# Gated linear attention with a soft mixture of experts: exchanging the two heads in half of y^T

## The chip, the cores and the metric

The kernel runs on one core of a Trainium2 chip. The metric is the device time of one execution in microseconds; the median of three runs of the kernel before is 186.47 us (186.04 to 186.61). A core has a matrix engine (TensorE, "PE" in the profile; its weight loads are listed as "PEld"), a vector engine (VectorE, DVE), a scalar engine (ScalarE, ACT), GpSimd (POOL), and a sync engine (SyncE, SP) that here issues all transfers. They work side by side and wait for each other by semaphores. Matrix results land in PSUM, whose banks hold 512 fp32 columns in each of 128 partitions; everything else is in SBUF.

## The reference

Everything is fp32. For each of 4 batches and 8 heads, over 768 tokens of head dimension 48:

```python
f = 1.0 / (1.0 + np.exp(-f_logit))
for t in range(S):
    state = f[:, :, t, :, None] * state + np.einsum('bhd,bhe->bhde', k[:, :, t], v[:, :, t])
    y[:, :, t] = np.einsum('bhd,bhde->bhe', q[:, :, t], state)
```

The eight heads of a token are put side by side into x, [3072 tokens, 384]. Then a soft mixture with 8 experts of 4 slots each (32 slots, hidden size 1024):

```python
logits = x @ phi                                   # [3072, 32]
d = softmax(logits, over tokens);  slot_input = d.T @ x
h = np.maximum(slot_input[e] @ w1[e], 0.0);  slot_out[e] = h @ w2[e]
c = softmax(logits, over slots);   out = c @ slot_out   # [3072, 384]
```

## The kernel before

The recurrence is done in chunks of 128 tokens (six chunks, `NM`), two heads at a time: 16 pairs of heads, four to a batch. Of a pair, head 0 lies in partitions 0 to 47 and head 1 in partitions 64 to 111 of 112. For each pair:

- the decays: e, ln, the scan `L` (`Lb`), g, p on ScalarE and VectorE, k and q scaled on GpSimd (`kb`, `qb`);
- `kt`: k turned to tokens by partitions, six transposes (L337), copied out by VectorE;
- `score` (L349): per chunk and head k^T q, with the 48 dimensions of a head in the rows, masked by VectorE into `scb`;
- `kv` (L377): the state that each chunk adds; `state` (L381) scans over chunks on VectorE into `sb`;
- `intra` (L368): y^T of each chunk from v and the masked scores, added up in PSUM with
- `inter` (L390): y^T from the state before the chunk and q, chunks 1 to 5, two heads each. Head r has its operands in rows 64r to 64r+47 and its output in partitions 64r to 64r+47;
- `y_copy`: y^T to `yT` in SBUF; `logits` (L413): phi times y^T, four groups of 192 tokens (a chunk and a half) in four strips of 32 output partitions, added up over the four pairs of a batch; `x_tr` (L401) and `x_copy`: y turned to tokens by partitions (`xb`).

Per batch follow the maximum and exponential of the logits, `l_tr` (twice: "te" for the weights of the slot inputs, "tl" for the softmax over slots), `slots_in` (L457, the slot inputs), a running join of the batches on VectorE, and the softmax over slots (`c_max` to `c_div`), which `c_tr` turns into `cT`. As a group of 192 tokens is a chunk and a half, `l_tr` does two transposes and two products with picked columns of the identity.

After the last batch comes the ending: `up` (L580), `turn`, `down` (L624) over all experts, and `combine` (L669), whose results are copied to a staging buffer and stored in two halves of 192 columns, six stores for each half.

The order of the work is written by a planner (`Plan`): each step is declared with an engine, an estimated duration, what it reads and writes, and a due time. Up to the last pair the order on each engine is that of the due times; loads on SP and the whole ending are ordered by simulated time. PSUM is divided into three buffers "a" of two banks and two buffers "b" of one bank; a step takes a free one by name, and the steps that read it free it. A mode such as "rows", "quarters" or "square" beside a step's name is the shape of tiles it uses on TensorE, for which the planner charges a change.

Of the kernel before, what the change touches and what calls it, by code (L numbers as in the profile page):

```python
# [28 lines left out]
PIECE = 768  # L29
HALF = DM // 2  # L30

# [170 lines left out]
def gla_soft_moe_kernel(ctx: ExitStack, tc: tile.TileContext, q, k, f, v, vt, phi, w1, w2, out):  # L202
# [46 lines left out]
    el = P([128, NM, NS], "el")  # L249
    ce = P([128, NM, NS], "ce")  # L250
    cm = P([128, NM], "cm")
    cT = P([128, 6, 128], "cT")
# [7 lines left out]
    phs = P([PW, PPB, NS], "phs")  # L260
# [16 lines left out]
    for t in pbx:  # L277
        nc.vector.memset(t[:, :, NM - 1], 0.0)

# [82 lines left out]

    def intra(o, i, h):
        u = unit(("y", i)) if h == 0 else un["y", i]
        for m in range(3 * h, 3 * h + 3):
            for r in range(2):
                vv = vb[i % N_V][:, m].rearrange("p r e -> p (r e)")[:, D * r : D * r + (D if r else 64)]
                nc.tensor.matmul(  # L368
                    u[rows(r), C * m : C * m + C], vv, scb[i % N_SC][:, r, h, m % 3],
                    start=m in (0, 4), stop=False, skip_group_check=True,  # L370
                )
# [13 lines left out]
    def inter(o, i):  # L385
        u = un["y", i]
        for m in range(1, NM):
            for r in range(2):
                rs = slice(64 * r, 64 * r + D)
                nc.tensor.matmul(  # L390
                    u[rs, C * m : C * m + C], sb[i % N_S][rs, :, m - 1], qb[i % N_Q][rs, C * m : C * m + C],
                    start=False, stop=m in (3, NM - 1), skip_group_check=True,
                )

    def y_copy(o, i):
        copy(o, yT[i % N_Y][:PW], un["y", i][:PW, :S])
# [6 lines left out]
    def x_copy(o, i):  # L403
        b, p = divmod(i, PPB)
        dst = xbs[b % 2][:, :, 96 * p : 96 * p + 96].rearrange("p m (r e) -> p m r e", r=2)
        copy(o, dst, un["xt", i][:, :S].rearrange("p (m r e) -> p m r e", m=NM, r=2)[:, :, :, :D])


    def logits(o, i):
        b, p = divmod(i, PPB)  # L410
        u = unit(("pl", b)) if p == 0 else un["pl", b]
        for g in range(4):
            nc.tensor.matmul(  # L413
                u[32 * g : 32 * g + 32, :192], phs[:, p], yT[i % N_Y][:PW, 192 * g : 192 * g + 192],
                start=p == 0, stop=p == PPB - 1, skip_group_check=True,
            )
# [11 lines left out]
    def l_tr(o, src, key):  # L428

        u = unit(key)  # L430
        pick = ident.rearrange("p (a b s) -> p a b s", a=2, b=2)
        nc.tensor.transpose(u[:, 0:128], src[:, 0:128], ident)
        nc.tensor.transpose(u[:, 224:352], src[:, 64:192], ident)
        for b, cs in ((0, slice(128, 192)), (1, slice(0, 64))):
            half = slice(64 * b, 64 * b + 64)
            nc.tensor.matmul(
                u[half, 128:256].rearrange("p (a x) -> p a x", a=2)[:, :, :NS], src[:, cs], pick[:, :, b], start=True, stop=True,
            )

    def by_block(key):  # L440
        return un[key][:, :384].rearrange("p (n a x) -> p a n x", n=3, a=2)[:, :, :, :NS]

    def blocks(t):
        return t.rearrange("p (a n) s -> p a n s", a=2)

    def el_copy(o, key):
        copy(o, blocks(el), by_block(key))

    def slots_in(o, b, key, rounds=(0, 1)):
# [3 lines left out]
        for x in rounds:  # L453
            for g in range(4):
                half = slice(64 * (g % 2), 64 * (g % 2) + 64)
                ws, n = (half, 1 + 3 * (g // 2)) if x else (slice(0, 128), 2 * (g % 2) + 3 * (g // 2))
                nc.tensor.matmul(u[32 * g : 32 * g + 32, :DM], el[ws, n], xb[ws, n], start=x == 0, stop=x == 1)  # L457
# [25 lines left out]
    def c_max(o, key):  # L483
        nc.vector.reduce_max(cm.rearrange("p (a n) -> p a n", a=2), by_block(key), axis=AX.X)

    def c_sub(o, key):
        m = cm.rearrange("p (a n) -> p a n", a=2).unsqueeze(3).broadcast_to([128, 2, 3, NS])
        nc.vector.tensor_tensor(blocks(ce), by_block(key), m, op=ALU.subtract)
# [4 lines left out]
    def c_sum(o):  # L493
        nc.vector.reduce_sum(cm, ce, axis=AX.X)
        nc.vector.tensor_scalar(cm, cm, 1e-9, None, op0=ALU.add)
        nc.vector.reciprocal(cm, cm)  # L496

    def c_div(o):
        nc.gpsimd.tensor_tensor(ce, ce, cm.unsqueeze(2).broadcast_to([128, NM, NS]), op=ALU.mult)  # L499

    def c_tr(o, b, key):

        u = unit(key)
        nc.tensor.transpose(u[:, :128], flat(ce)[:, :128], ident)
        if b % 2:
            nc.tensor.matmul(u[64:, 128:256], flat(ce)[:, 128:], ident, start=True, stop=True)
        else:
            nc.tensor.transpose(u[:64, 128:256], flat(ce)[:, 128:], ident)

    def c_copy(o, b, key):  # L510
        u = un[key]
        copy(o, cT[:, b], u[:, :128])
        rs = slice(64 * (b % 2), 64 * (b % 2) + 64)
        copy(o, cT[rs, 4 + b // 2], u[rs, 128:256])
# [141 lines left out]
    of = out.rearrange("b n p d -> p (b n) d")  # L656

    def staged(k0, k1):
        t = w1b[4 + k0 // 8]
        return t[:, 2 * HALF * (k0 % 8) : 2 * HALF * ((k1 - 1) % 8 + 1)].rearrange("p (n d) -> p n d", d=HALF)  # L660

    def combine(o, hh, u2):

        u = unit(("pf", hh, u2)).rearrange("p (n d) -> p n d", n=2)
        b, x = divmod(u2, 3)
        for n in range(2):
            g = 2 * x + n if x < 2 else 2 * (b % 2) + n
            gs = slice(32 * g, 32 * g + 32)
            nc.tensor.matmul(  # L669
                u[:, n, :HALF], cT[gs, b if x < 2 else 4 + b // 2], s4[gs, HALF * hh : HALF * hh + HALF],  # L670
                start=True, stop=True,
            )

    def out_copy(o, hh, u2):
        n = 12 * hh + u2
        copy(o, staged(n, n + 1), un["pf", hh, u2].rearrange("p (n d) -> p n d", n=2)[:, :, :HALF])

    def store(o, hh, u0, u1):
        n = 12 * hh
        nc.sync.dma_start(of[:, 2 * u0 : 2 * u1, HALF * hh : HALF * hh + HALF], staged(n + u0, n + u1))  # L680
# [10 lines left out]
    def attention(i):  # L691
# [17 lines left out]
        op("dk", {"POOL": 1.84}, decay_k, i, r=[G, K], w=[K], due=z - 2 * T + 3.8)  # L709
# [13 lines left out]
        op(("ie", "quarters"), {"PE": 1.13}, inter, i, r=[Q, SB, YY], w=[YY], due=z + 2.2, ni=40)  # L723
# [5 lines left out]
    def soft(b, z):  # L729

        CT, tl = ("ct", b), ("tl", b)
        op(("tl", "square"), {"PE": 0.35}, l_tr, lt, tl, r=["lt"], w=[tl], due=z[0], take=[(tl, "a")], ni=12)
# [5 lines left out]
        op(("ct", "square"), {"PE": 0.35}, c_tr, b, CT, r=["ce"], w=[CT], due=z[1], take=[(CT, "a")], ni=6)  # L738
# [4 lines left out]
    def mixture(b, z):  # L743
# [8 lines left out]
        op(("te", "square"), {"PE": 0.35}, l_tr, et, key, r=["et"], x=["el"], w=[key], due=z + T + 4, take=[(key, "b")], ni=12)  # L752
# [7 lines left out]
        op(("pi", "strips"), {"PE": 1.3}, slots_in, b, key, r=[*XB[b], "el"], w=[key], due=z + 3 * T + 3.5, take=[(key, "b")], ni=32)  # L760
# [6 lines left out]
    op("lphi", {"SP": 0.45}, load, phs, phi, w=["phs"], due=5, kb=56)  # L767
# [57 lines left out]
    op(("pi", "strips"), {"PE": 1.3}, slots_in, L, PI, r=[*XB[L], "el"], w=[PI], due=z + 2, take=[(PI, "b")], ni=32)  # L825
# [31 lines left out]
    for hh in range(2):  # L857
# [10 lines left out]
        for u2 in range(12):  # L868
            b, x = divmod(u2, 3)
            key, d2 = ("pf", hh, u2), d + 5 + 0.3 * u2  # L870
            cts = [("cT", b)] if x < 2 else [("cT", 2 * (b // 2)), ("cT", 2 * (b // 2) + 1)]
            op("comb", {"PE": 0.35}, combine, hh, u2, r=[("s4", hh), *cts], w=[key], due=d2, take=[(key, "a")], ni=8)
# [129 lines left out]
```

## Time and profile before

| | us |
|---|---|
| median of three runs | 186.47 |
| profiled execution | 185.44 |
| its span, first to last instruction | 183.6 |
| TensorE busy | 159.2 |
| VectorE / ScalarE / GpSimd busy | 108.3 / 95.7 / 93.1 |
| score, both calls (L349) | 27.3 |
| intra (L368) / inter (L390) | 25.8 / 21.4 |
| kv (L377) / kt (L337) / xt (L401) | 15.0 / 13.3 / 12.0 |
| logits (L413) / slot inputs (L457) | 8.5 / 6.5 |

The lower rows are TensorE's busy times by line over the whole span; overlapping instructions count once. The span leaves out what lies before the first and behind the last instruction, 1.8 us. The profile names lines as L390, an instruction's tiles as out<-in, and x20 is a count of instructions. An fp32 product appears as two matmul records, a transpose as one. In the chain of work that ended last, pieces follow each other in time, each with its start and length; "issue" is time in which an engine waited for nothing that the profile shows.

### The profile page before, as it was taken

Reading aid. Unit: us, or ns where it says so; the run is one execution under the profiler, and the core shown is the slowest. Engines: PE = TensorE matmul, PEld = TensorE weight load, DVE = VectorE, ACT = ScalarE, POOL = GpSimd, SP = SyncE. Lnnn points to the kernel's source line nnn. Section 1 sums busy time; section 2 is a strip of 40 time slices with the busy share of each in tenths; the row PEclk is TensorE's granted clock in tenths of the full one; section 3 lists DMA queues with packets and bytes.
Section 4 is the critical chain, followed back from the end, with each engine's and each line's share of the span. In section 5 each row is a group of like instructions: output and inputs, shape, how many; then the busy total and the mean of one; then the engine's idle time right before and its main releaser. Section 6 shows DMA issues by size and latency. Waiting matters only on the chain.

```text
span 183.6 us, 5864 instructions
## 1 busy us (share of the span) xinstructions
PE 159.2 (87%) x2468; PEld 123.2 (67%) x2468; DVE 108.3 (59%) x154; ACT 95.7 (52%) x171; POOL 93.1 (51%) x88
## 2 busy tenths in 40 slices
PE   0049999999899999999999999999999999997800
PEld 0049889889688796898876888878645446665600
DVE  2669878678977684889967677749261113032300
ACT  4975666856777466695775663512252211052610
POOL 2199999988657939676896788520101000000000
PEclk9999999999999999999999999999999999999985
DMA  5999999999999999997566459999996194059691
GB/s 197 378 405 379 303 349 346 411 398 401 390 396 398 396 403 396 397 321 231 170 209 177 153 153 289 354 376 388 384 381 263 25 305 190 4 167 301 213 315 54
DMA packets 24931, 54.00 MB, mean 294 GB/s; under 512 B 2256, under 2 KB 8512, under 8 KB 24896
## 3 DMA queue, kind: packets, MB, share of 16 engines
q1 hardware_dynamic: 24896, 53.54, 81.7%
q8 instruction: 21, 0.34, 0.8%
q14 instruction: 14, 0.11, 0.2%
HBM read 48.82 MB, written 4.72 MB: 292 GB/s over the span
## 4 chain that ended last, share of the span: by engine, by line
PE 81%; issue 5%; DVE 3%; DMA 2%; POOL 2%; ACT 2%; SPq 0%; DVEq 0%; POOLq 0%; ACTq 0%
PE sc L349 14%; PE y L368 12%; PE y L390 10%; PE kv L377 7%; PE po L624 6%; PE up L580 6%; PE kt L337 5%; PE xt L401 5%; PE pl L413 4%; PE pf L669 4%; PE pi L457 3%; DMA kb<-in_k_dram 2%; DVE same L284 1%; PE turn L597 1%; ACT w1b L295 1%
## 5 line engine op out<-in xcount | busy, mean ns | idle before, releaser
L319 POOL TENSOR_TENSOR kb<-kb,gb 112x768 f32<-112x768 f32 x16 | 40.0, 2500 | 16.8 <-ACT gb L312 15.7
L309 DVE TENSOR_TENSOR_SCAN Lb<-starts,fb 112x768 f32<-112x768 f32 x16 | 29.9, 1870 | 5.7 <-ACT fb L305 5.6
L323 POOL TENSOR_TENSOR qb<-qb,pb 112x768 f32<-112x768 f32 x16 | 29.6, 1851 | 5.9 <-ACT pb L315 5.9
L354 DVE TENSOR_TENSOR scb<-sc,mask 128x768 f32<-128x768 f32 x32 | 29.1, 950 | 5.5 <-PE sc L349 5.4
L295 ACT COPY yT<-y 112x768 f32<-112x768 f32 x16 | 12.8, 799 | 34.6 <-PE y L390 34.6
L349 PE MATMUL sc<-qb,kb 48*128 48x128 f32 x384 | 27.3, 290 | 2.3 <-issue 1.2
L349 PEld LDWEIGHTS sc<-qb,kb 48*128 48x128 f32 x384 | 24.1, 196 | 5.1 <-issue 1.8
L368 PE MATMUL y<-scb,va 128*48 128x128 f32 (+1 forms) x384 | 25.8, 278 | 0.1
L295 DVE COPY kta<-kt 128x672 f32<-128x672 f32 x16 | 13.7, 853 | 19.8 <-PE kt L337 19.8
L337 PE MATMUL kt<-ident,kb 112*128 112x112 f32 x96 | 13.3, 277 | 11.2 <-POOL kb L319 11.2
L368 PEld LDWEIGHTS y<-scb,va 128*64 128x64 f32 (+1 forms) x384 | 21.9, 131 | 0.4 <-issue 0.2
L390 PE MATMUL y<-qb,sb 48*48 48x128 f32 x320 | 21.4, 277 | 0.0
L390 PEld LDWEIGHTS y<-qb,sb 48*48 48x48 f32 x320 | 17.9, 160 | 2.7 <-DVE sb L381 2.2
L337 PEld LDWEIGHTS kt<-ident,kb 112*128 112x128 f32 x96 | 9.9, 146 | 14.4 <-POOL kb L319 11.5
L499 POOL TENSOR_TENSOR ce<-ce,cm 128x192 f32<-128x192 f32 x4 | 4.6, 1154 | 21.8 <-DVE cm L496 13.8
L305 ACT ACTIVATE fb<-fb,one 112x768 f32<-112x768 f32 x16 | 15.0, 937 | 0.6
L377 PE MATMUL kv<-va,kta 128*64 128x48 f32 (+1 forms) x384 | 15.0, 225 | 0.0
L302 ACT ACTIVATE fb<-fb 112x768 f32<-112x768 f32 x16 | 13.4, 840 | 2.9 <-DMA fb<-in_f_dram 2.9
L377 PEld LDWEIGHTS kv<-va,kta 128*64 128x64 f32 (+1 forms) x384 | 13.0, 135 | 2.0 <-issue 0.2
L332 POOL COPY pbx<-pb 112x240 f32<-112x240 f32 x16 | 14.3, 892 | 0.0
L315 ACT ACTIVATE pb<-Lb 112x768 f32<-112x768 f32 x16 | 13.5, 845 | 0.0
L295 ACT COPY xb<-xt 128x576 f32<-128x576 f32 x16 | 10.2, 638 | 6.2 <-PE xt L401 6.2
(145 smaller groups left out, 245.7 us busy)
## 6 DMA issues: line engine op xcount, KB each, us to landing
w1b<-in_w_dram SPq DMA_DIRECT2D x34, 384.0 KB, 6.8
fb<-in_f_dram SPq DMA_DIRECT2D x16, 384.0 KB, 6.1
kb<-in_k_dram SPq DMA_DIRECT2D x16, 384.0 KB, 6.6
qb<-in_q_dram SPq DMA_DIRECT2D x16, 384.0 KB, 6.2
va<-in_v_dram SPq DMA_DIRECT2D x16, 288.0 KB, 6.3
out_dram<-w1b SPq DMA_DIRECT2D x12, 384.0 KB, 4.0
scb<-in_w_dram SPq DMA_DIRECT2D x4, 384.0 KB, 6.3
fb<-in_w_dram SPq DMA_DIRECT2D x3, 384.0 KB, 4.6
```

The lines of the kernel that those rows point to most:

```text
L295: {"ACT": nc.scalar.copy, "DVE": nc.vector.tensor_copy, "POOL": nc.gpsimd.tensor_copy}[o.eng](dst, src)
L305: nc.scalar.activation(fb[i % N_F][:PW], fb[i % N_F][:PW], AF.Ln, bias=one[:PW])
L309: nc.vector.tensor_tensor_scan(Lb[i % N_L][:PW], flat(starts)[:PW], fb[i % N_F][:PW], 0.0, op0=ALU.mult, op1=ALU.add)
L319: nc.gpsimd.tensor_tensor(t, t, gb[i % N_G][:PW], op=ALU.mult)
L323: nc.gpsimd.tensor_tensor(t, t, pb[i % N_P][:PW], op=ALU.mult)
L332: nc.gpsimd.tensor_copy(pbx[i % N_S][:PW, :, : NM - 1], ends(i)[:, : NM - 1].unsqueeze(1).broadcast_to([PW, D, NM - 1]))
L337: nc.tensor.transpose(u[:, C * m : C * m + PW], kb[i % N_K][:PW, C * m : C * m + C], ident[:PW, :PW])
L349: nc.tensor.matmul(u[:, 512 * r + C * m : 512 * r + C * m + C], kb[i % N_K][rs, cs], qb[i % N_Q][rs, cs], start=True, stop=True,)
L354: nc.vector.tensor_tensor(scb[i % N_SC][:, :, h], un["sc", i, h].rearrange("p (r x) -> p r x", r=2)[:, :, : 3 * C].rearrange("p r (m t) -> ...
L368: nc.tensor.matmul(u[rows(r), C * m : C * m + C], vv, scb[i % N_SC][:, r, h, m % 3], start=m in (0, 4), stop=False, skip_group_check=True,)
L377: nc.tensor.matmul(u[rows(r), :, m], ktb[i % N_KT][:, m, rows(r)], vb[i % N_V][:, m, r], start=True, stop=True)
L390: nc.tensor.matmul(u[rs, C * m : C * m + C], sb[i % N_S][rs, :, m - 1], qb[i % N_Q][rs, C * m : C * m + C], start=False, stop=m in (3, NM ...
```

## The change

In chunks 0 to 2 the two heads change places in y^T: head 0 goes to partitions 64 to 111, head 1 to 0 to 47. `intra` writes them there, and `inter` does so too, so its products use the tiles (rows 0-63 to columns 64-127) and (rows 64-127 to columns 0-63) in chunks 1 and 2 and the two others in chunks 3 to 5, in the order 1, 3, 2, 4, 5. y in PSUM has three chunks in each bank (before: four and two).

What reads y^T has to follow. phi is loaded in two versions (112 KB, before 56 KB), with the heads either way. The two odd groups of 192 tokens are put into another order, the whole chunk first and the shared half chunk behind, so `logits` writes them in two products. Now the second half of each group is a half chunk, `l_tr` is three plain transposes; the weights get eight blocks of 32 columns (before six), of which the softmax over slots zeroes the unused halves with a mask `valid`. `slots_in` undoes the exchange: the two groups of exchanged chunks are written as two products of half the columns each. `c_tr` is always two transposes, `c_copy` one copy instead of two. `combine` takes whole chunks by 32 rows as before and shared chunks by 64 rows. The output is laid out as [128, 2, 24, 192], so that a store writes 3072 adjacent bytes per partition; the host puts the tokens back in order. The tl turn takes a buffer b instead of a, and some planned durations differ.

```diff
+SWAP = NM // 2
+WHOLE, SHARED = (0, 2, 3, 5), (1, 4)
...
+    el = P([128, 2, 4, NS], "el")
+    ce = P([128, 8, NS], "ce")
+    cT = P([128, B, 2, 128], "cT")
...
+    nc.gpsimd.memset(valid, 1.0)
+    nc.gpsimd.memset(valid[64:, 4:8:2], 0.0)
+    nc.gpsimd.memset(valid[:64, 5:8:2], 0.0)
...
     def intra(o, i, h):
...
             for r in range(2):
+                at = 1 - r if m < SWAP else r
+                v0 = 576 * (i % N_V) + 96 * m + D * r
                 nc.tensor.matmul(
-                    u[rows(r), C * m : C * m + C], vv, scb[i % N_SC][:, r, h, m % 3],
-                    start=m in (0, 4), stop=False, skip_group_check=True,
+                    u[rows(at), y_cols(m)], va[:, v0 : v0 + (D if at else 64)], scb[i % N_SC][:, r, h, m % 3],
+                    start=m % 3 == 0, stop=False, skip_group_check=True,
                 )
...
     def inter(o, i):
-        for m in range(1, NM):
+        for m in (1, 3, 2, 4, 5):
             for r in range(2):
                 rs = slice(64 * r, 64 * r + D)
+                at = 64 * (1 - r if m < SWAP else r)
                 nc.tensor.matmul(
-                    u[rs, C * m : C * m + C], sb[i % N_S][rs, :, m - 1], qb[i % N_Q][rs, C * m : C * m + C],
+                    u[at : at + D, y_cols(m)], sb[i % N_S][rs, :, m - 1], qb[i % N_Q][rs, C * m : C * m + C],
...
     def logits(o, i):
-        for g in range(4):
-            nc.tensor.matmul(
-                u[32 * g : 32 * g + 32, :192], phs[:, p], yT[i % N_Y][:PW, 192 * g : 192 * g + 192],
+        for x in range(2):
+            for g in range(4):
+                t = 192 * g
+                to, at, n = (0, t + 64, C) if g % 2 else (0, t, 192)
+                if x:
+                    if g % 2 == 0:
+                        continue
+                    to, at, n = C, t, 64
+                nc.tensor.matmul(
+                    u[32 * g : 32 * g + 32, to : to + n], phs[:, int(g < 2), p], yT[i % N_Y][:PW, at : at + n],
...
     def l_tr(o, src, key):
         nc.tensor.transpose(u[:, 0:128], src[:, 0:128], ident)
-        nc.tensor.transpose(u[:, 224:352], src[:, 64:192], ident)
-        for b, cs in ((0, slice(128, 192)), (1, slice(0, 64))):
-            nc.tensor.matmul(
-                u[half, 128:256]..., src[:, cs], pick[:, :, b], start=True, stop=True,
-            )
+        nc.tensor.transpose(u[:, 128:256], src[:, 64:192], ident)
+        nc.tensor.transpose(u[:64, 128:256], src[:, 128:192], ident)
...
     def slots_in(o, b, key, rounds=(0, 1)):
...
         for x in rounds:
+            for r in range(2):
+                for g in range(4):
+                    ws, n = (half, SHARED[g // 2]) if x else (slice(0, 128), WHOLE[g])
+                    dst, src = u[32 * g : 32 * g + 32, :DM], xb[ws, n]
+                    if g < 2:
+                        dst = dst.rearrange("p (w r e) -> p w r e", w=PPB, r=2)[:, :, r]
+                        src = src.rearrange("p (w r e) -> p w r e", w=PPB, r=2)[:, :, 1 - r]
+                    elif r:
+                        continue
+                    nc.tensor.matmul(dst, el[ws, x, g], src, start=x == 0 and r == 0, stop=x == 1, skip_group_check=True)
...
     def c_sum(o):
+        nc.vector.tensor_tensor(cm, cm, valid, op=ALU.mult)
...
     def c_tr(o, b, key):
-        nc.tensor.transpose(u[:, :128], flat(ce)[:, :128], ident)
-        if b % 2:
-            nc.tensor.matmul(u[64:, 128:256], flat(ce)[:, 128:], ident, start=True, stop=True)
-        else:
-            nc.tensor.transpose(u[:64, 128:256], flat(ce)[:, 128:], ident)
+        for x in range(2):
+            nc.tensor.transpose(u[:, 128 * x : 128 * x + 128], flat(ce)[:, 128 * x : 128 * x + 128], ident)
...
+    def store(o, hh, u2):
+        nc.sync.dma_start(out[:, hh, 2 * u2 : 2 * u2 + 4], staged(hh, u2, 2))
...
-        op("dk", {"POOL": 1.84}, decay_k, ...
+        op("dk", {"POOL": 2.5}, decay_k, ...
-        op(("ie", "quarters"), {"PE": 1.13}, inter, ...
+        op(("ie", "quarters"), {"PE": 0.72}, inter, ...
-        op(("tl", "square"), {"PE": 0.35}, l_tr, ..., take=[(tl, "a")], ni=12)
+        op(("tl", "square"), {"PE": 0.35}, l_tr, ..., take=[(tl, "b")], ni=6)
-    op("lphi", {"SP": 0.45}, load, phs, phi, w=["phs"], due=5, kb=56)
+    op("lphi", {"SP": 0.45}, load, phs, phi, w=["phs"], due=5, kb=112)
```

The path for large decays (`general`), which these inputs do not take, is adapted in the same way.

114 lines of the change are left out of this document (51 added, 63 removed).

## Prediction

> **What bounds the kernel now.** I read the page first: the busy shares, the slices and the chain that ended last.
>
> ```profile
> span 183.6 us, 5864 instructions
> PE 159.2 (87%) x2468; PEld 123.2 (67%) x2468; DVE 108.3 (59%) x154; ACT 95.7 (52%) x171; POOL 93.1 (51%) x88
> PE   0049999999899999999999999999999999997800
> PE 81%; issue 5%; DVE 3%; DMA 2%; POOL 2%; ACT 2%; SPq 0%; DVEq 0%; POOLq 0%; ACTq 0%
> ```
>
> TensorE (PE) is busy in nearly every slice from the fourth to the 38th and owns 81% of the chain. Only the start (waiting for the first loads and elementwise work) and the end (draining stores) lie outside it. So I next read the chain in order of time, one steady pair of heads:
>
> ```profile
> 75.93 1.27 PE y L390 x20
> 77.19 0.46 PE pl L413 x8
> 77.66 0.73 PE kt L337 x6
> 78.38 0.57 PE xt L401 x6
> 78.96 1.54 PE sc L349 x24
> 80.49 0.77 PE kv L377 x21
> 81.26 1.39 PE y L368 x24
> 82.65 1.27 PE y L390 x20
> ```
>
> A pair takes 6.72 us (75.93 to 82.65) and consists of TensorE work without a hole; the first number is the start, the second the length on the chain. What is taken off a TensorE piece here comes off the time, 16 times, until another engine's loop becomes the longer one.
>
> **The inter products, 16 times.** Ten fp32 products are 20 matmul records. Head 0 now goes from rows 0-47 to output partitions 0-47, head 1 from rows 64-111 to partitions 64-111: the diagonal pair of 64x64 tiles only. Narrow windows of the timeline show what runs at once:
>
> ```profile
> 75.86 0.46 PE L390 MATMUL y<-qb,sb 48*48 48x128 f32 x4
> 75.86 0.57 PE L390 MATMUL y<-qb,sb 48*48 48x128 f32 x6
> 77.12 0.37 PE L413 MATMUL pl<-yT,phs 112*32 112x192 f32 x4
> 69.87 0.53 PE L457 MATMUL pi<-xb,el 64*32 64x384 f32 x4
> 72.17 0.38 PE L349 MATMUL sc<-qb,kb 48*128 48x128 f32 x2
> ```
>
> Two more records of the inter product lengthen the stretch by 0.11 us (first two rows): one round of the two diagonal tiles. Five products per tile are ten rounds, 1.10 of the 1.27 us; 0.17 is entry. After the change chunks 1 and 2 leave crosswise and chunks 3 to 5 straight, in the order 1, 3, 2, 4, 5, so the straight tiles have three products (six rounds) and the crossed ones two, beside them: 0.17 + 6 x 0.11 = 0.83 us, 0.44 less.
>
> Do four such tiles run together? The last three rows are the nearest. Four records of column strips stand in 0.37 us, though one alone takes 0.34 (the mean of that group below): all four at once. The 64x32 records of the slot inputs run four at once with two row halves, so two tiles that share rows but not columns do not exclude each other. The score's two row halves write the same partitions in two banks at once, so sharing columns does not either. The new y also has chunks 0 to 2 in one bank and 3 to 5 in the other. Bounds per pair: 0 (no overlap) and 0.63, if 20 records go at the pace of kv, 24 in 0.77 us. I take 0.44, since no row suggests a third tile would wait: **-7.0 us**.
>
> The Trainium skill speaks against this: "TensorEngine Tiling (Array Packing)", Restrictions and Gotchas, says that different row tiles cannot access the same PSUM bank simultaneously. Chunks 1 and 2 send both row halves to one bank, so by that rule two of the four tiles would wait and the term would be about 0. But the kernel does so already: both heads of a chunk go to one bank in different partitions, and four records stand in 0.46 us above, two per round. The trace does not bear the rule out for disjoint partitions.
>
> **Extra records.** The logits get 12 records instead of 8: strips 1 and 3 split 192 columns into 128 and 64 because their halves need different head orders. Slot inputs get 24 instead of 16 with half the columns in strips 0 and 1.
>
> ```profile
> L413 PE MATMUL pl<-yT,phs 112*32 112x192 f32 x128 | 8.5, 338 | 0.0
> ```
>
> No strip streams more columns than before, and the strips overlap, so the lower bound is 0. The upper one is four (eight) records at a serial transpose's 0.12 us (kt: six in 0.73), 0.48 and 0.96. It is nearest to the lower one; I take 0.05 per logits and 0.1 per slot input: 16 x 0.05 + 4 x 0.1 = **+1.2 us**.
>
> **Turning the logits and weights, plain transposes.** Eight turns (tl and te, four batches) lose four matmul records with 64 columns and get one transpose; two of four ct turns lose a two-record matmul.
>
> ```profile
> 61.44 0.26 PE tl L432
> 61.81 0.27 PE tl L436 x4
> 62.08 0.73 PE kt L337 x6
> 70.97 0.11 PE ct L508
> 71.08 0.58 PE kt L337 x6
> 101.26 0.36 PE ct L506 x2
> ```
>
> The removed group costs 0.27, and kt behind it takes 0.73 against 0.58 behind a 64-wide transpose (ct L508), the form that is added at 0.11: 0.27 - 0.11 + 0.15 = 0.31, times 8 = **-2.5**. The odd ct gives 0.36 - 0.11 + 0.15 = 0.40, twice: **-0.8**. Bounds for the two together: 0.16 and 0.25 alone, if the 0.15 has another reason (-1.8), to the -3.3 taken.
>
> **The PSUM buffer of tl.** It moves from the three large buffers (a) to the two small ones (b). Today tl, kt and xt hold all three when the scores want one:
>
> ```profile
> PE sc L349 <- issue: 1.2, 3, 0.4
> 62.84 0.86 DVE L295 COPY kta<-kt 128x672 f32<-128x672 f32 x1 [1.77 <-PE kt L337]
> 63.80 1.61 PE L349 MATMUL sc<-qb,kb 48*128 48x128 f32 x24 [0.42 <-issue]
> 63.99 0.36 DVE L488 TENSOR_TENSOR ce<-tl,cm 128x192 f32<-128x192 f32 x1
> ```
>
> The scores start 0.10 after kt's copy ends (63.70), with 0.42 idle; three such places, 1.2 us. With one large buffer free they go: **-1.2**. In b, tl lies between two kv products and must be read by c_sub before the next one; c_sub is done at 64.35 (last row), a microsecond before the scores end and kv begins (63.80 + 1.61). If that cover were gone, kv would wait for the rest of the DVE work.
>
> **What is late next.**
>
> ```profile
> L309 DVE TENSOR_TENSOR_SCAN Lb<-starts,fb 112x768 f32<-112x768 f32 x1 | 1.7, 1733 | 0.0
> L381 DVE TENSOR_TENSOR_SCAN sb<-kv,pbx 112x288 f32<-112x288 f32 x1 | 0.7, 747 | 0.0
> L354 DVE TENSOR_TENSOR scb<-sc,mask 128x768 f32<-128x768 f32 x32 | 29.1, 950 | 5.5 <-PE sc L349 5.4
> ```
>
> VectorE's loop per pair (the Lb scan 1.73, kt copy 0.86, two masks 1.90, state scan 0.75; means in the rows) is 5.3 us. The circle from one state scan to the next runs over inter 0.83, logits 0.51, kt 0.73, xt 0.57, half a score 0.77, two masks and the scan: 6.1 us and some 0.1 for handovers, against a new pair of 6.72 - 0.44 + 0.05 = 6.33. It just fits, so part of the gain comes back wherever VectorE has more to do:
>
> ```profile
> PE sc L349 <- DVE kta L295: 0.7, 1, 0.7
> 83.92 1.72 DVE L464 TENSOR_TENSOR nmb<-nmx,nmb 128x1 f32<-128x1 f32 x1
> 116.97 1.50 DVE L474 SCALAR_TENSOR_TENSOR sms<-sms,nmb 128x1 f32<-128x1 f32 x1
> 53.55:83.91 30.36, 29.94 (x484) 24.87 (x486) 21.44 (x27) 20.90 (x36) 23.33 (x27) 1.00 1.01 378
> 83.91:114.61 30.70, 30.28 (x484) 24.93 (x487) 23.39 (x32) 19.14 (x34) 24.35 (x19) 1.00 0.65 197
> ```
>
> In the pair with the copies for `same` TensorE already waits 0.7 for VectorE, so its 0.44 is lost. The joins are held 1.5 to 1.7 by GpSimd work running over them (one column takes that long); three such pairs lose about 0.2 each and the one near 117 another 0.3. In three tl pairs the masks come behind c_max and c_sub, a third wider now, about 0.15 each. Together **+1.8** (bounds 0 and 5, a whole 0.31 in each of 16 pairs). Over a batch (the last two rows, four pairs in 30.4 and 30.7 us; the columns are TensorE, weight loads, VectorE, ScalarE, GpSimd, clock, DMA share, GB/s) VectorE has 21 to 23 us, ScalarE 19 to 21, GpSimd 23 to 24: none near the 28 that remain.
>
> **The end.** Output is stored as rows of 3072 bytes instead of four of 768.
>
> ```profile
> 174.62 0.48 ACT w1b L295
> out_dram<-w1b SPq DMA_DIRECT2D x12, 384.0 KB, 4.0
> 176.00:177.00 1.00, 0.00 (x0) 0.00 (x0) 0.00 (x0) 0.00 (x0) 0.00 (x0) 1.00 1.04 318
> 60.00:70.00 10.00, 9.58 (x156) 7.58 (x156) 7.28 (x11) 6.17 (x10) 7.07 (x6) 1.00 1.04 399
> ```
>
> The last copy ends at 175.10, then only stores run, at 318 GB/s with all DMA engines busy (share 1.04), while loads in rows of 3072 bytes reach 399 at the same share. The last six stores are 2.36 MB: 7.4 us at 318, 5.9 at 399. The copies deliver them faster than either. Bounds 0 (writes are slower anyway) and -1.5; share 1.04 in both rows says that packets and not the memory fill the time, so **-1.4**. "DMA: Bandwidth & Descriptors", Specifications, of the Trainium skill puts line rate at 512 bytes or more; by it 768 would already be full rate, the term 0 and the time 178.0. The two rows differ by a quarter.
>
> **Costed at nothing.** The phi load grows by 56 KB (0.15 us at 399 GB/s) and lands long before the first logits. Three small memsets sit on GpSimd's queue ahead of its first multiplication, where it waits for ScalarE; uncovered, some 0.5. The wider ScalarE and GpSimd steps of the mixture and the extra multiplication by `valid` have a pair of slack; the one copy of cT instead of two saves ScalarE 0.1, off the path. The combine keeps its records. GpSimd's new planned cost of 2.5 can reorder only loads and the ending; on SP no load is moved past another in a pair. The DMA engines are full in the second batch (share 1.01) because weights fill the gaps between the pairs' loads, and at 0.65 in the third, so the faster pairs find room. If a reordered load came late, a pair would wait about 1 us.
>
> **The sum.** -7.0 + 1.2 - 3.3 - 1.2 + 1.8 - 1.4 = -9.9. The profiled execution took 185.44 us; less 9.9 is 175.5. The median of the runs, 186.47, is 1.03 above it, so I predict **176.6 us**.
>
> **Rivals.** (A) The four tiles run two at a time. The inter term is 0, and with it the 1.8 that comes back: -4.7, 181.8 us. Against it stand the rows of strips and halves; the tiling page's rule would end here. 9%.
>
> (B) VectorE's circle becomes the bound: with 0.13 to spare per pair, handovers that are 0.4 longer in all make a pair 6.6 instead of 6.33, 14 times: +3.8, 180.4 us. For it speaks how little is to spare, against it that VectorE's own sum is only 5.3. 14%.
>
> (C) Slower: changing between the straight and the crossed pair of tiles costs a drain, as changing the shape of tiles does (0.15, the two kt rows). There are three changes per pair, 48 in all; with no overlap left the sum is -4.7 + 48 x price. It decides from 0.098 us on; at 0.15 it is +2.5, 189.0 us. Against it: the strips change tile at every record and lose nothing. 7%, 2 of them at a price that comes out even.
>
> **How the numbers follow.** The forecast has 70%, A 9, B 14, C 7. Its own range is 174 to 179, from the bounds of the turns, extra records, stores and give-back; below lies kv's pace of inter (-3.0 more). With A and B the range is 173.5 to 182.0; C and the edges are left out. A time within 0.3% (0.56 us) cannot be told from no change. Faster: 70 + 9 + 14 = 93; same 2; slower 5.
>
> **What would show it.** In the profile after: the inter piece at 0.83 on the chain (1.27 refutes the overlap, 1.7 is C); logits at 0.5; tl without the fourfold group and kt behind it at 0.58; no wait of scores on "issue" in the tl pairs; pairs of about 6.3; waits of the inter product or masks on VectorE that grow (B); stores near 400 GB/s behind the last copy. It would be wrong above all if the ending were put in another order by the planner with holes of a microsecond, or if loads arrived late in the faster pairs.

## The result, and the profile after

The kernel after takes **179.08 us** (median of 4 runs, 179.03 to 179.20) against 186.25 for the kernel before in the same sitting (186.01 to 186.61): ratio 0.9614, 95% interval 0.9595 to 0.9634. That is 7.2 us less; 9.9 less were forecast, 176.6 us, with a range of 173.5 to 182.0.

The page of the kernel after, the lines that answer to the first ones shown of before:

```profile
span 177.3 us, 6018 instructions
PE 153.5 (87%) x2538; PEld 123.0 (69%) x2538; DVE 111.8 (63%) x161; ACT 94.6 (53%) x164; POOL 94.0 (53%) x91
PE   0039999999899999999999999999899999987830
PE 77%; DVE 6%; issue 4%; POOL 4%; ACT 4%; DMA 2%; POOLq 0%; DVEq 0%; ACTq 0%
```

TensorE still bounds the kernel: as busy as before in share, 5.7 us less in time, with more records (2538, before 2468). The last slices read 87830 where before had 97800: TensorE has holes near the end. The chain of waits, one steady pair of heads:

```profile
31.83 0.84 PE y L407 x20
32.67 0.47 PE pl L439 x8
33.14 0.72 PE kt L347 x6
33.86 0.57 PE xt L418 x6
34.44 1.54 PE sc L359 x24
35.98 0.77 PE kv L393 x21
36.75 1.38 PE y L384 x23
38.13 0.84 PE y L407 x20
```

A pair is 6.30 us, 31.83 to 38.13 (forecast 6.33, before 6.72). The inter piece (first row) is 0.84 for 20 records, the logits 0.47 against 0.46 before although they have four records more (x8 counts those on the chain; over the whole span it is 192 records after 128). A pair with the turn of the logits (tl), on the same chain, and the waits of the scores:

```profile
60.11 0.26 PE tl L457
60.37 0.11 PE tl L458
60.48 0.11 PE tl L459
60.59 0.58 PE kt L347 x6
PE sc L359 <- DVE kta L305: 1.2, 1, 1.2
```

The group of four records is gone, the key transposes behind it take 0.58 and not 0.73, and the scores no longer wait on "issue" (before three times, 1.2 us together). What is left is one wait for VectorE, 1.2 us, in the pair with the copies for `same`; before it was 0.7.

To see where in the span the time went, I read the same places on both chains: the second pair's scores, the first `up`, the second `so` (the last exchange step before the final combines). First before, then after:

```profile
20.78 1.54 PE sc L349 x24
139.79 1.83 PE up L580 x13
168.83 0.61 PE so L635 x2
```

```profile
21.83 1.54 PE sc L359 x24
131.75 1.90 PE up L600 x13
162.88 0.61 PE so L655 x2
```

| stretch | before | after | difference |
|---|---|---|---|
| start of the span to scores of pair 1 | 20.78 | 21.83 | +1.05 |
| from there to `up` | 119.01 | 109.92 | -9.09 |
| `up` to the second `so` | 29.04 | 31.13 | +2.09 |
| second `so` to the end of the span | 14.77 | 14.42 | -0.35 |
| span | 183.6 | 177.3 | -6.3 |

The long middle gave more than was forecast for it, and the ending took 2.1 us back. The profiled execution of after took 179.07, its median; that of before was 0.8 below its own, which is why the spans differ by less than the medians. (The first `up` instruction of before starts at 139.72, 0.07 ahead of its piece on the chain; counted from there, the ending took back 2.0 us.) The ending of after, and its last stretch by windows (columns: window, length, TensorE busy, weight loads, VectorE, ScalarE, GpSimd, granted clock, DMA share, GB/s):

```profile
151.17 0.26 PE tl L457
...
154.40 0.55 PE pf L688 x8
...
154.97 0.49 ACT w1b L305
...
155.59 0.41 PE ct L531 x2
156.00 0.55 PE pf L688 x8
...
156.57 0.57 DVE w1b L305
```

```profile
168.00:169.00 1.00, 1.00 (x8) 1.00 (x8) 0.33 (x1) 0.48 (x1) 0.00 (x0) 0.50 1.02 393
```

Three things stand here. The combines (`pf`) of the first half come in a row and wait for the copies that free their PSUM buffers; before, they stood between the pieces of down (`po`), three combines (12 records) at a time. The last batch's tl and ct, which were ahead of `up` before, are in the ending. And the last combines ran at a granted clock of 0.50, eight records in a microsecond. The stores reached 393 GB/s against 318 before.

### The profile page after: what moved, and what is told of

Read it like the earlier page. It is cut to its first block, busy times and chain, and to the rows that moved or that the text cites. A ratio compares the mean times of both kernels' runs of the same rounds, so it can differ in the third digit from the quotient of the medians.

```text
span 177.3 us, 6018 instructions
## 1 busy us (share of the span) xinstructions
PE 153.5 (87%) x2538; PEld 123.0 (69%) x2538; DVE 111.8 (63%) x161; ACT 94.6 (53%) x164; POOL 94.0 (53%) x91
## 4 chain that ended last, share of the span: by engine, by line
PE 77%; DVE 6%; issue 4%; POOL 4%; ACT 4%; DMA 2%; POOLq 0%; DVEq 0%; ACTq 0%
PE sc L359 13%; PE y L384 13%; PE y L407 7%; PE kv L393 6%; PE po L644 6%; PE up L600 6%; PE kt L347 5%; PE pf L688 5%; PE xt L418 4%; PE pl L439 3%; POOL ce L525 2%; DMA fb<-in_f_dram 2%; PE pi L482 2%; DVE same L294 1%; PE turn L617 1%
## 5 line engine op out<-in xcount | busy, mean ns | idle before, releaser
L329 POOL TENSOR_TENSOR kb<-kb,gb 112x768 f32<-112x768 f32 x16 | 41.3, 2582 | 13.7 <-ACT gb L322 12.8
L333 POOL TENSOR_TENSOR qb<-qb,pb 112x768 f32<-112x768 f32 x16 | 30.1, 1881 | 4.5 <-ACT pb L325 4.5
L364 DVE TENSOR_TENSOR scb<-sc,mask 128x768 f32<-128x768 f32 x32 | 29.1, 951 | 4.1 <-PE sc L359 4.0
L384 PE MATMUL y<-scb,va 128*64 128x128 f32 (+1 forms) x384 | 27.1, 285 | 0.4 <-DVE scb L364 0.4
L525 POOL TENSOR_TENSOR ce<-ce,cm 128x256 f32<-128x256 f32 x4 | 5.1, 1272 | 41.8 <-DVE cm L522 41.2
L384 PEld LDWEIGHTS y<-scb,va 128*64 128x64 f32 (+1 forms) x384 | 23.3, 135 | 1.0 <-issue 0.5
L407 PE MATMUL y<-qb,sb 48*48 48x128 f32 x320 | 14.6, 285 | 0.0
L322 ACT ACTIVATE gb<-Lb 112x768 f32<-112x768 f32 x16 | 13.2, 828 | 0.0
L407 PEld LDWEIGHTS y<-qb,sb 48*48 48x48 f32 x320 | 11.1, 162 | 2.9 <-DVE sb L397 2.2
```

Source lines behind the costliest of these rows:

```text
L329: nc.gpsimd.tensor_tensor(t, t, gb[i % N_G][:PW], op=ALU.mult)
L333: nc.gpsimd.tensor_tensor(t, t, pb[i % N_P][:PW], op=ALU.mult)
L364: nc.vector.tensor_tensor(scb[i % N_SC][:, :, h], un["sc", i, h].rearrange("p (r x) -> p r x", r=2)[:, :, : 3 * C].rearrange("p r (m t) -> ...
L384: nc.tensor.matmul(u[rows(at), y_cols(m)], va[:, v0 : v0 + (D if at else 64)], scb[i % N_SC][:, r, h, m % 3], start=m % 3 == 0, stop=False ...
L407: nc.tensor.matmul(u[at : at + D, y_cols(m)], sb[i % N_S][rs, :, m - 1], qb[i % N_Q][rs, C * m : C * m + C], start=False, stop=m in (2, 5) ...
```

## The experiments

The theory after this profile: the middle is the change as forecast; what is missing lies in the ending, in the order that the planner made, and at the two ends in the clock. The rival: the inter products gave less than 7.0, and something else hides it. Where no other kernel is named, the differences of the first four are against the kernel before at 186.16 us.

**The inter products alone.** The kernel before with only this (and with y's chunks three to a bank), so that two chunks get the other head's inter part:

```diff
-        for m in range(1, NM):
+        for m in (1, 3, 2, 4, 5):
             for r in range(2):
+                at = 64 * (1 - r if m < 3 else r)
-                    u[rs, C * m : C * m + C], sb[...][rs, :, m - 1], ...
+                    u[at : at + D, y_cols(m)], sb[...][rs, :, m - 1], ...
```

> The kernel before with the crossed inter products alone (order 1, 3, 2, 4, 5; y in PSUM three chunks to a bank); the rest does not follow, so the heads of chunks 1 and 2 get each other's inter part. If the four tiles run together and the pair is bound by TensorE, the inter piece is 0.84 us and the time 186.3 - 7.0 + about 1.8 given back = 181.1 us (180 to 182). If the gain of the whole change came from the turns, buffers and stores instead, the inter piece stays at 1.27 and the time at 186.3. If VectorE's circle were already the bound, inter is 0.84 but the pair stays near 6.6 and the time is above 183.

Measured: 179.68 us (178.92 to 180.31), ratio 0.9641 (0.9603 to 0.9678), 6.5 less, and 1.4 less than expected. Its chain:

```profile
51.55 0.84 PE y L395 x20
61.72 0.42 issue
```

The piece is 0.84, and the wait behind tl is still there, as it should be without the other buffer. From the starts of the scores, pair for pair, 14 of the 15 stretches from pair 1 to `up` are 0.41 to 0.43 shorter than in the kernel before; the one with the copies for `same` gains nothing. So the inter products give nearly their whole 0.43 each time, and by themselves most of the result; of the 1.8 that were to be given back, this kernel shows the 0.43 at `same` alone.

**The order of the chunks.** The kernel after with one line changed:

```diff
-        for m in (1, 3, 2, 4, 5):
+        for m in (1, 2, 3, 4, 5):
```

> The changed kernel with the chunks of the inter products in the order 1, 2, 3, 4, 5: the same tiles, results and number of products, but two products of the crossed tiles stand before those of the straight ones. If matmuls start strictly in order, only two tiles run at a time, the inter piece goes back to 1.2 us or more and the time to 179.1 + 5.2 = 184.3 us (183 to 186). If the engine picks a later matmul whose tile is free, the piece stays at 0.84 and the time at 179.1.

Measured: 179.02 us (178.92 to 179.29), ratio 0.9621 (0.9589 to 0.9653), the same as after:

```profile
51.77 0.86 PE y L407 x20
```

Two crossed chunks in succession want the same two tiles, and taken strictly in turn the stretch would be two rounds of 0.11 longer. It is 0.02 longer. The order of issue is not what makes the four tiles run together.

**The stores alone.** The kernel before with the output in rows of 3072 bytes:

```diff
-        nc.sync.dma_start(of[:, 2 * u0 : 2 * u1, HALF * hh : HALF * hh + HALF], staged(n + u0, n + u1))
+        nc.sync.dma_start(out[:, hh, 2 * u0 : 2 * u1], staged(n + u0, n + u1))
```

> The kernel before with the output laid out so that a store writes 3072 adjacent bytes per partition, nothing else. If the stores behind the last copy are bound by the size of their packets, the DMA rate there rises from 318 to some 390 GB/s and the time falls by 1.4 to 1.7 us, to 184.7. If writes are as fast as they can be, or the end is set by something else (the branch behind the last copy), it stays at 186.3.

Measured: 184.68 us (184.08 to 185.23), ratio 0.9922 (0.9892 to 0.9952): 1.5 less, as the forecast had it. Its profile shows 0.6 to 1.0 of that where the stores are. From the second `so` to the end it takes 14.14 us, against 14.77 in the profile of before, whose last combines ran at full clock, and 15.09 in that of w0 (below), where they ran partly at half clock, as here. Behind the last copy the stores run at 373 GB/s. Where the rest of the 1.5 comes from is not shown; the times of the kernel before alone spread over 1.4 us.

**The ending's order.** The kernel after with the combine steps declared without a mode, as before. The planner charges for a change of mode, and the two modes "pf0" and "pf1" had made it group them:

```diff
-            op(("comb", "pf" + str(u2 // LAST)), {"PE": 0.35}, combine, ...
+            op("comb", {"PE": 0.35}, combine, ...
```

> The changed kernel with the combine steps declared without a mode of tiles, as before, so that the planner puts them between the down products again; nothing else differs. If the ending lost about 2 us of the gain because eight combines of the first half stand in a row and wait for their copies, the time falls by 1.3 to 2.5 us, to 177.2 (176.5 to 177.8), and the second sum of slots ('so') starts 7.5 us or more before that of the kernel before instead of 5.95. If those waits only moved work that has to be done anyway, it stays at 179.1.

Measured: 176.73 us (176.47 to 178.57), ratio 0.9528 (0.9487 to 0.9569): 2.35 less than after, and faster than both kernels. The chain of waits:

```profile
17.55 1.32 PE y L384 x23
...
152.99 0.85 PE pf L688 x12
153.84 0.79 PE po L644 x16
154.62 0.85 PE pf L688 x12
...
156.26 1.18 PE pf L688 x12
...
159.38 1.06 PE pf L688 x12
```

The combines alternate with down again without a hole. The last two rows are the shared chunks, whose combines use 64 rows: twelve such records take 1.18 us, eight by 32 rows with four by 64 take 1.06, and twelve by 32 rows 0.85, as all did before. But the first row shows that this execution was also luckier at the start: its first intra took 1.32 us, and 2.59 in the profile of after, with the same work. The six times fall into two groups (176.5 to 176.8 and 178.1 to 178.6). What the order is worth could not be read from the medians.

**A filler at the start.** For that the start had to be made alike. In four kernels 38 transposes without use fill TensorE's idle start: before (w0), after (w1), after with the plain combines (w2), and after with tl in the large PSUM buffers as before (u1):

```diff
+    op("warm", ..., warm, 24, ident, ...)
+                op("warm", ..., warm, 8, Lb[0][:PW], ...)
+                op("warm", ..., warm, 6, gb[0][:PW], ...)
```

> The kernel before, with 38 transposes without use put into TensorE's idle time ahead of the first key transposes, so that TensorE isn't idle for the first 11 us of the span. What it tells apart: the lengths of intra(0) on the chain of the kernels so far were 1.6 to 2.9 us in executions with the same work, at a recorded clock of 1.00. Theory 1 (a start that depends on what TensorE did in the microseconds before): with the filler the scores of pair 0 (24 records) take about 1.6 us and not 2.9, intra(0) about 1.3 to 1.5 us, the milestone sc(1) comes 0.5 to 1 us earlier than in the kernel before, and the time is 185.2 to 185.7 (186.2 less that). Rival: the slow start doesn't hang on earlier work; then the same 2.9 us, and the time stays at 186.2 within 0.3, or is some tenths longer by the filler.

> The kernel after, with the same filler at the start. Theory 1: its pair 0 loses the 1.5 to 2.3 us by which its scores and intra(0) ran longer than in the fourth experiment (intra(0) 1.32 us there, 3.0 here): 177.0 to 177.8 us. The difference to the kernel before with the filler is then the change without the luck of the start: about -8 us, near what the milestones between sc(1) and the second `so` gave. Rival (the start stays as it is, or VectorE's first scan bounds pair 0 and not TensorE): 178.8 to 179.3, and the difference to the kernel before with the filler stays at -7.2.

Measured: w0 186.16 us (184.60 to 186.50), w1 178.90 (178.29 to 179.45): the same as without it. My theory of the start fell in this form, since the first scores still took 2.94 and 2.86 us. The windows of TensorE say why (window, length, TensorE busy, granted clock, DMA share, GB/s), w1:

```profile
6.00:7.00 1.00, 0.93 (x7) 1.00 0.99 344
12.00:13.00 1.00, 0.11 (x2) 1.00 1.05 415
13.00:14.00 1.00, 0.91 (x8) 0.60 1.02 400
20.00:21.00 1.00, 1.00 (x22) 0.99 0.99 356
```

The filler's own transposes got twice as fast at 6.4 us, so the clock had risen; it fell to 0.50 at 13.2, as the scores began, after three and a half microseconds with six transposes in them, and rose again at 20.0. The Trainium skill, "TensorE: Matmul & The Clock Gate", section "What's actually happening", says that the gate is set by windows of 3.4 us that run free of the kernel; here 6.4, 13.2 and 20.0 are two such windows apart (6.8), so the trace agrees.

> The fourth experiment (the kernel after, its combine steps declared without a mode, so that the planner puts them between the down steps again) with the filler. It prices the order of the ending without the luck of the start. Theory: the ending of the kernel after costs 1 us (of the 2.1 us by which its stretch from `up` to the second `so` is longer than before, the rest is tl(3), ct(3) and the flag that moved there): the kernel after with the filler less 0.7 to 1.5 us, 176 to 176.8. Rival 1 (all of the 2.35 us of the fourth experiment were the ending): less 2 us or more. Rival 2 (all of it was the start): the same time as the kernel after with the filler, within 0.3.

Measured: 177.49 us (176.49 to 178.25), ratio 0.9556 (0.9495 to 0.9617), 1.4 less than w1, with its start again lucky in the profile. The stretch from `up` to the second `so`, where no clock changes, is the firm number: 30.04 us against 31.13 in w1. The order of the combines costs 1.1 us.

> The kernel after with the filler, with the one PSUM buffer choice undone: the turned logits tl are put into the large kind of buffer again, as before the change. Theory (the prediction's term of 1.2 us): the three waits of the scores behind tl (0.33 to 0.44 us each in the kernel before) come back, and the time is the kernel after with the filler plus 0.7 to 1.2 us. Rival (the buffers aren't what these scores waited for, or VectorE takes the gain at those three pairs, where the waits for kta are 1.2 us in sum in the kernel after): plus 0 to 0.3 us, with the waits for kta shorter by what the new ones cost.

Measured: 178.83 us (177.39 to 179.85), the same as w1 (178.90). By the time the rival would be right; the profile says otherwise. On the chain of u1 the wait ahead of the scores is there again; on that of w1 the scores start as the transposes end:

```profile
118.91 0.10 PE flag L674
119.01 0.33 issue
```

```profile
117.48 0.57 PE xt L423 x6
118.06 1.54 PE sc L364 x24
```

The three pairs with a tl are 0.48, 0.49 and 0.47 us longer in u1 than in w1, 1.44 together (the pairs around them take 0.3 of it back), so the buffer is worth what was forecast. But with tl in the large buffers the planner left tl(3) and ct(3) ahead of `up`; the combines stay in a row (on its chain 0.55, 0.62 and 2.52 us behind one piece of down), and it takes 30.05 us from `up` to the second `so`. From the scores of pair 1 it lost 1.4 us ahead of `up` and won 1.1 behind it.

**A denser filler.** 68 transposes, the last 8 between the first key transposes and the first scores, so that no idle stretch comes before these:

```diff
-    warm, 24, ident    +    warm, 30, ident
-    warm, 8, Lb[0]     +    warm, 16, Lb[0]
-    warm, 6, gb[0]     +    warm, 14, gb[0]
+                op("warm", ..., warm, 8, gb[0][:PW], ..., due=-T + 4.8, ...)
```

> The kernel before with a denser filler at the start: 30 + 16 + 14 + 8 transposes without use instead of 24 + 8 + 6, the last 8 between the first key transposes and the first scores. With the thin filler the recorded clock rose to 1.00 at 5.3 us, fell to 0.50 at 12.5 us, after three microseconds with few matmuls, and rose again at 18.9. Theory: the clock follows the work of the microseconds just before; with no such gap it stays at 1.00 when the scores start at 13.1, these take 1.5 us and not 2.9, sc(1) comes at 19.5 to 20 us and not at 21.5, and the time is 184.6 to 185.3, with little spread at the start. Rival: the fall at 12 to 13 us has nothing to do with gaps; then the same profile, and 186.1 within 0.4.

Measured: 184.58 us (184.38 to 185.25), ratio 0.9938 (0.9914 to 0.9962): 1.5 less, and the two groups of times are gone. The granted clock rises at 5.3 us, where the filler's transposes begin to follow each other in half the time, and does not fall again before the scores of pair 1, which stand 1.2 us earlier than in w0 (21.55). The chain:

```profile
20.33 1.54 PE sc L354 x24
```

> The kernel after with the denser filler. Theory: sc(1) at 19.3 to 19.7 us instead of 21.5 to 21.8, where VectorE's first masks and scan bound pair 0; time 176.8 to 177.6. The difference to the kernel before with the same filler is then the change without the start's clock: main loop -9.05 (from sc(1) to `up`, the thin filler's two profiles), pair 0 -0.2 to -0.4, ending +2.0, stores -1.5: -8.0 to -9.0 us in all, against the -7.2 of the plain pair of kernels. Rival: the -7.2 stand, and what the profiles showed of the start cancels somewhere later: 177.3 to 178 with the kernel before at 184.6 to 185.3.

Measured: 177.31 us (176.69 to 178.19), 7.3 less than v0 (ratio of the medians 177.31 / 184.58 = 0.961); by the fastest runs 7.7. With the start at full clock in both, the change is worth what the plain kernels showed. My 8 to 9 was too much: two things that the thin filler's profiles could not show take it back.

```profile
19.66 1.54 PE sc L364 x24
...
21.20 0.90 PE kv L398 x22
22.10 1.70 PE y L389 x23
```

```profile
46.00:48.00 2.00, 0.84 (x14) 1.00 1.02 381
48.00:50.00 2.00, 2.00 (x37) 0.59 1.03 406
```

In pair 1 kv and intra stretch to 0.90 and 1.70 (0.77 and 1.38 in a steady pair): with TensorE at full clock this early, VectorE holds it. The scan of `Lb` ahead of that pair's masks takes 2.64 us here (1.75 in a steady pair), the masks come late, and the pair is 6.75 us, its whole gain lost. (In v0 that scan takes 2.62, and the pair is 6.72 us, as long as any.) And in this execution, the slowest of the six, the clock fell to half behind the wait for `same` (windows), which made that pair 1.6 us longer.

> The same with the combine steps declared without a mode. The stretch from `up` to the second `so` was 31.13 us in both profiles of the kernel after and 30.03 in the two of this order: 1.1 us less than the kernel after with the denser filler, 175.7 to 176.5. Rival (the 1.1 us are waited for again behind the second `so`, where the stores end the kernel): 0 to 0.4 less.

Measured: 175.62 us (175.41 to 177.23), ratio 0.9478 (0.9437 to 0.9520), 1.7 less than v1; five of the six runs lie within 175.4 and 176.3. From `up` to the second `so` 30.03 us, as in w2.

**tl of the last batch.** The same, and the last tl alone takes a large buffer:

```diff
-        op(("tl", "square"), ..., take=[(tl, "b")], ni=6)
+        op(("tl", "square"), ..., take=[(tl, "b" if b < B - 1 else "a")], ni=6)
```

> The same as the one before, and the last batch's turned logits (tl of batch 3) take the large kind of PSUM buffer, as all did before the change; by that its planner leaves tl(3) and ct(3) ahead of `up` instead of putting them among the down steps. Theory: 0.48 and 0.41 us of TensorE leave the ending, which falls from 30.03 to 29.1 us, and the stretch ahead of `up` grows by 0.2 at most, as it did in the kernel with all four tl in large buffers (13.66 against 13.46 us): 0.6 to 0.9 us less than the one before, about 175.2. Rival (the last tl and ct wait where they stand ahead of `up`): the same time within 0.3.

Measured: 175.56 us (175.05 to 176.44), ratio 0.9454 (0.9416 to 0.9491). It is the fastest median, and not to be told from v2. tl(3) and ct(3) do stand ahead of `up`, but the ending fell to 29.66 only, 0.37 less, where 0.9 was expected. Behind it the last combines, first v2, then v3:

```profile
163.37 2.54 PE pf L693 x22
```

```profile
163.03 3.88 PE pf L693 x22
```

In v3's profile they fell into a stretch at half clock, which took the gain back; whether that is so in most of its runs stays open.

## Why the prediction was right, and where its sum was off

The range, the sign and the mechanism held: the four tiles run together, and rivals A (two at a time, 181.8), B (VectorE's circle, 180.4) and C (a drain at each change of tiles, 189.0) did not come. The time was 2.5 us above the forecast. Term by term:

- **Inter, -7.0.** Right: 1.27 to 0.84, 0.43 in each pair, where 0.44 was forecast; alone, 6.5 less. The rule of the Trainium skill, "TensorEngine Tiling (Array Packing)", Restrictions and Gotchas, that different row tiles cannot access the same PSUM bank simultaneously, would have left nothing; for disjoint partitions the trace does not bear it out (0.84 us), as the prediction held.
- **Extra records, +1.2.** Mis-sized: the logits grew from 0.46 to 0.47, the slot inputs not at all (1.42 to 1.43 on the chain both times). It was some 0.15. These strips, at work together, took the extra records for next to nothing.
- **Turns, -3.3.** Right where they could be seen alone: 0.16 in the piece and 0.15 in the key transposes behind it, and pairs with a te 0.29 to 0.31 shorter in u1 than with the inter products alone. The odd ct, too, is right in its own pieces: ct and the key transposes behind it take 0.44 + 0.58 where they took 0.26 + 0.36 + 0.72, 0.32 less for the 0.40 forecast. But its pair became only 0.07 shorter than with the inter products alone (8.27 us in w1 after 8.34), and the first pair with slot inputs 0.24 longer. The prediction gave the wider steps of the mixture "a pair of slack". They have none: in both pairs the chain of after runs through GpSimd's multiplication `ce`, for which ct waits, and intra takes 1.46 us and not 1.38. The first of them:

```profile
66.38 1.91 POOL ce L525
68.33 0.44 PE ct L531 x2
```

- **tl's buffer, -1.2.** Right in place and size (1.44 less 0.3, from u1 and w1).
- **Given back to VectorE, +1.8.** The `same` pair gave back its 0.44 as forecast (1.2 of waiting after 0.7), and with the start at full clock pair 1 would too. The joins took theirs as well, but one stretch later than the te. Up to the scores behind a te nothing is lost. From there to the scores behind the tl, u1 (tl in the old buffer) is 0.31 shorter than with the inter products alone in the first batch, where nothing has to be joined yet, and only 0.02 and 0.01 in the next two. So in these two the 0.31 of the turn went to VectorE, 0.6 together, where 0.9 was forecast for the joins. Only these two of the three te pairs have a join. In the first of the two, after shows the loss in scores of 1.81 us, where before had 1.54 (at 86.31):

```profile
82.86 0.87 PE sc L359 x12
83.73 0.94 PE sc L359 x12
```

Taken with the terms above, the stretch from pair 1 to `up` was forecast at 15 x -0.44 + 1.2 - 3.3 - 1.2 + 1.8 = -8.1 and came to -9.1.

- **Stores, -1.4.** Right by the medians when alone (-1.5); the profiles show 0.7 to 1.1. The Trainium skill, "DMA: Bandwidth & Descriptors", Specifications, puts line rate at 512 bytes or more; that is not enough here, as 768-byte rows gave 318 GB/s and 3072-byte rows 393. In the kernel after, from the second `so` to the end, it is 14.42 us, and 15.09 (w0) and 15.13 (inter products alone) with the old stores, all three with combines at half clock: 0.7. With the last combines at full clock it is 13.59 (v1) and 13.88 (w1) after 14.71 (v0) and 14.77 (before), about 1.0.
- **Costed at nothing: the ending.** This is the step that failed. The text named a new order by the planner, "with holes of a microsecond", as what would make it wrong above all, and gave it no price. It cost 2.1 us. From `up` to the second `so` the four orders that the planner made of the new ending take, in us:

| | tl(3), ct(3) ahead of `up` | among the down steps |
|---|---|---|
| combines between the downs | 29.66 (v3) | 30.04, 30.03 (w2, v2) |
| combines in a row | 30.05 (u1) | 31.13 (w1, v1) |

The old ending takes 29.1 (w0, v0). So the two orders together cost 1.5, and more than each by itself (0.4 each): the row costs 1.1 (w1 against w2) when tl(3) and ct(3) are in the ending too. Ahead of `up` these two had cost almost nothing: u1, which keeps them there, takes 13.66 us from the last scores to `up`, w1 13.46. What even v3 keeps, 0.55, fits a term that the prediction put at nothing because "the combine keeps its records": the four shared combines of the first half, by 64 rows, lengthen two pieces from 0.85 to 1.06 and 1.18, 0.54 together. No run undoes that, so this part is read from the chains alone.

- **Not in the sum: the start.** Pair 0 was counted like the others. In the profile of after its scores took 2.93 us, as before, and its intra 2.59 (before 1.56), at half the rate; from its scores to those of pair 1 it was 8.53 us against 7.83 before, where 0.43 less was due.

From the middle, the ending and the stores as measured, -9.1 + 2.1 - 0.7 = -7.7; the start adds between -0.4 and +0.7, by the window in which the clock rises. The -7.2 lies within it. Of the 2.7 us that are missing, the ending is the part that is shown, 2.1 us, with 1.1 of it undone by one line and 1.5 by two; the records that cost nothing made up a microsecond, and the stores and the start hold the rest. How that rest is shared in a given run stays open: v0 and v1, with the start at full clock in both, still differ by 7.3, since v1 loses its gain in pair 1 and in some executions at `same`.

## What to carry to other kernels

Where pairs of matmuls use only the two diagonal quarters of the array, let half of the work leave crosswise: on this TensorE-bound chain the gain was the whole of the cut, 0.43 us of 6.72 in all pairs but one. When steps are put in order by a planner, a new mode or another buffer is a change of the whole order: compare the order of the ending before costing it at nothing. Cost a product by its shape and not by its count of records, when the shape sets how many run together. And before comparing two kernels within a per cent, see at which clock their first and last matmuls ran.

## What the runs showed of the hardware

- The order in which matmuls of different tiles are issued did not matter: with two in succession on the same tiles the stretch took 0.86 us, with them apart 0.84.
- TensorE's rate at the start is twofold: in the profiles without filler the records took twice as long until a moment between 17.4 and 20.2 us from the span's start, while the clock column had 1.00 throughout. It showed 0.50 only in stretches behind an earlier rise (w1 at 13 to 20 us).
- A few microseconds of sparse work were enough for half clock: at 13.2 us in w1 (six transposes between 9.8 and 13.2), at 48 us in v1 behind the wait for `same` (14 records in two microseconds), and in the last combines of nine of the fourteen profiles, where a piece of 22 records takes 3.7 to 4.0 us and not 2.54.
- Twelve records of the combines took 0.85 us by 32 rows and 1.18 by 64 rows, with the same 192 columns each.
